# Pair differences of the later batches taken on GpSimd, with three smaller edits, in a fused attention and hardswish kernel

## The chip, the cores and the metric

The kernel runs on one core of a Trainium2 chip. The metric is the device time of one execution in microseconds (us); before the change it was 329.49 us, the median of three runs (325.65 to 331.78). A core has five engines, each with its own in-order instruction queue: TensorE (PE, with its weight loads shown apart as PEld), VectorE (DVE), ScalarE (ACT), GpSimd (POOL) and SyncE (SP). They meet only through semaphores, so an instruction that waits holds back all that is behind it on its engine.

## The reference

`x` has 4 batches of 12480 rows of 128 numbers; `inducing` has 32 rows. All is fp32.

```python
def mab(q, kv):
    s = scale * (q @ kv.transpose(0, 2, 1))
    a = np.exp(s - s.max(-1, keepdims=True))
    a /= a.sum(-1, keepdims=True) + 1e-09
    return a @ kv
h = mab(I, x)              # 32 rows H a batch, from all rows of x
y = mab(x, h)              # each row of x: a weighted mean of those 32 rows
u = y @ w_in               # 128 -> 2048
g = u * np.clip(u + 3.0, 0.0, 6.0) / 6.0
out = g @ w_out            # 2048 -> 128
```

## The kernel before, in words

A row of `y` is a mean of the 32 rows of H with weights p, so `u` is the same mean of the 32 rows of G = H @ w_in. As long as no element of G passes 3 in size, g is the quadratic u (u + 3) / 6, and the square of a mean is the mean of the squares less a sum over pairs of p_m p_n (G_m - G_n)^2. So the kernel never forms `u`. Once a batch it makes a linear matrix L (from hardswish of G) and a quadratic one Cq, with a row for each of 512 features that hold the pairs; each row of the output is then one matmul of its weights with L (through the block matrix BD) and one of its 512 pair products with Cq, divided by its denominator. Conditions that this rests on (sizes of G and of the denominators) are counted as the kernel runs; where one fails, a slow direct path at the end computes everything again.

**Rows.** A batch is 7 groups: 6 of 2048 rows and one of 192. A group is worked on in chunks of 512 rows, 25 chunks a batch, 100 in all.

**What a chunk does (the main loop).** b_base makes the feature exponentials TF in two halves (PE L652, ScalarE L659), two chunks ahead; b_spread loads d, a copy of dk spread over partitions (SP, L639), four ahead; b_prod multiplies the two into TD (VectorE L668), one ahead. Then PE runs b_lin (L676, opens the output bank) and four b_quad (L692, 16 matmuls), with b_r between (L612, denominators, reciprocal on VectorE L613). b_evac (VectorE L708) scales the output one chunk later; SP writes it out a whole group at a time (L715). Once a group b_pack, b_e and b_f (L623, L579, L593) make dk and the normalised weights.

**Preparation of the next batch.** While batch b runs, the units of batch b+1 stand in one list and are woven into the chunks at three points of each (`bg`), a share of the list in proportion to the chunks done. Before the change each unit counts one, whatever it does; some are empty and only space others out. The list has a part on x (a_units): transposes a_T (L260, copied out at L261), scores a_s1 (L268), aggregation a_agg (L282, which also issues the next loads of x on POOL's queue, L118), casts to bf16 (L251). Then comes the coefficient part (c_units):
- c_sum, c_den, c_HT: the softmax sum (dred, L362), H, its transpose HT, rounded copies HTb and HTr, the differences dH of rows of H (VectorE L399, L400), and the coefficients W and Wd of the features.
- c_sq, sixteen times, one for each block jb of 128 columns of w_in: a matmul of dH with w_in (L470) gives the 512 differences of G in PSUM; ScalarE squares them (L481) into `sq`, of which SQB = 12 buffers exist.
- c_G beside it: a matmul of the fp32r HTr with w_in (L414) for G itself.
- c_C, sixteen times: sq times w_out into Cq's bank (L490). It lies twelve units behind c_sq.
- c_hs, c_L, c_BD: hardswish of G, L and BD (L424, L426, L444, L460, L464). c_tail scales Cq (L503, L505).

Batch 0 has nothing to hide under: a_first and c_first prepare it in a row, about the first 46 us.

**End.** After the last chunk's matmuls VectorE counts five conditions (L793 to L806), PE and VectorE add them up into bad_i (L810 to L814), then comes the last b_evac. Every engine loads bad_i and branches over the direct path, whose code is written out four times, once a batch, with three hardware loops in each.

Of the kernel before, what the change touches and what calls it, by code (L numbers as in the profile page):

```python
# [24 lines left out]
TG = 16  # L25
SL = 4
XBUF = 5
SQB = 12
LEAD = 2


def shifted(t, off, k_step, i_step):

    a = t[:, 0, 0:1]
    return bass.AP(
        tensor=a.tensor, offset=a.offset + off, ap=[a.ap[0], [k_step, 2], [1, 32], [i_step, 4]]
    )


@with_exitstack  # L40
def kernel(
# [35 lines left out]
    keep = ctx.enter_context(tc.tile_pool(name="keep", bufs=1))  # L77
    bad_i = keep.tile([1, 1], I32, name="bad_i")

    with ExitStack() as es:  # L80
# [15 lines left out]
        sqp = es.enter_context(tc.tile_pool(name="sqp", bufs=SQB))  # L96
        coef = es.enter_context(tc.tile_pool(name="coef", bufs=2))
        PSUM = bass.MemoryType.PSUM
        psF = es.enter_context(tc.tile_pool(name="psF", bufs=5, space=PSUM))
# [42 lines left out]
        w_in_b = const.tile([P, F], BF16, name="w_in_b")  # L142
        w_in_r = const.tile([P, F], FP32R, name="w_in_r")
        w_out_b = const.tile([P, FB, C], BF16, name="w_out_b")
        w_out_r = const.tile([P, FB, C], FP32R, name="w_out_r")
# [8 lines left out]

        ident = const.tile([P, P], FP32, name="ident")
        make_identity(nc, ident[:, :])
# [146 lines left out]
        def a_units(b):  # L303

            us = []
            late = []
            for g in range(NGR):
                box = {}

                def s1_unit(g=g, box=box):  # L310
                    a_s1(b, g)
                    box["a1"] = S[b]["a1"]

                def first(g=g):
                    a_T(b, g, 0)
                    if g + 1 < NGR:
                        a_cast(b, g + 1, ((nc.scalar.copy, 0, 2),))

                def second(g=g):
                    a_T(b, g, 1)  # L320
                    if g + 1 < NGR:
                        a_cast(b, g + 1, ((nc.scalar.copy, 2, 4),))

                us.append(first)
                if late:
                    us.append(late.pop(0))
                us.append(second)
                us += late
                us.append(s1_unit)
                late = [  # L330
                    lambda g=g, box=box: a_agg(b, g, 0, box["a1"]),
                    lambda g=g, box=box: a_agg(b, g, 1, box["a1"]),
                ]
            return us + late

# [49 lines left out]
        def c_HT(b):  # L385
# [7 lines left out]
            nc.scalar.copy(st["HTb"][:, :], htp[:, :M])  # L393
            st["HTr"] = cst.tile([P, M], FP32R, name="HTr")
            nc.scalar.copy(st["HTr"][:, :], htp[:, :M])
            dH = cst.tile([P, 2, 2, M, 4], BF16, name="dH")
            st["dH"] = dH

            nc.vector.tensor_sub(dH[:, 0], shifted(HT, 0, 1, 0), shifted(HT, 2, 0, 4))  # L399
            nc.vector.tensor_sub(dH[:, 1], shifted(HT, 1, -1, 0), shifted(HT, 4, 0, 4))  # L400
            W = coef.tile([P, 2, M, 4], BF16, name="W")
# [6 lines left out]
        def c_G(b, lo, hi):  # L408
# [4 lines left out]
            for jb in range(lo, hi):  # L413
# [4 lines left out]
                )  # L418

        def c_hs(b):  # L420
            st = S[b]
            gp = st["gp"]
            r6 = cst.tile([P, 512], FP32, name="r6")
            nc.vector.tensor_scalar(r6[:, :], gp[:, :], 3.0, 0.0, op0=ALU.add, op1=ALU.max)  # L424
# [42 lines left out]
        def c_sq(b, jb):  # L467
# [8 lines left out]
            if b == 0 and jb % 4 == 1:  # L476
                d32 = cst.tile([P, 512], FP32, name="d32")
                nc.vector.tensor_copy(d32[:, :], dpm[:, :])
# [29 lines left out]
        def c_units(b):  # L508
            gap = [lambda: None]
            cs = [lambda jc=jc: c_C(b, jc) for jc in range(FB)]  # L510
            ls = [lambda: c_hs(b), lambda: c_L(b, 0), lambda: c_L(b, 1), lambda: c_BD(b)]
            us = [lambda: c_sum(b)] + gap + [lambda: c_den(b)] + gap + [lambda: c_HT(b)] + 3 * gap

            us += [lambda jb=jb: (c_sq(b, jb), c_G(b, jb, jb + 1)) for jb in range(SQB)]
            for jb in range(SQB, FB):
                us += [cs[jb - SQB], lambda jb=jb: (c_sq(b, jb), c_G(b, jb, jb + 1))]
            us += ls[0:1] + cs[4:6] + ls[1:3] + cs[6:8] + ls[3:] + cs[8:]
            return us + [lambda: c_tail(b)]

        def c_first():  # L520
# [13 lines left out]
            for c in range(4):  # L534
                b_spread(0, c)
            load_held(3, len(held))
            for jb in range(3, 7):
                sq(jb)
# [162 lines left out]
        def b_evac(b, c, op):  # L701
# [10 lines left out]
            )  # L712
            if (j + 1) * SL == n:
                r0 = b * N + t0
                nc.sync.dma_start(  # L715
                    out[r0 : r0 + p * n, :].rearrange("(p i) c -> p i c", i=n), ot[:p, :n, :]
                )

# [12 lines left out]
        for b in range(1, B):  # L731
            for i, h in enumerate((0, 2)):
                ahead.setdefault(max((b - 1) * NCK + i - 2, 0), []).append(
                    lambda b=b, h=h: a_cast(b, 0, ((nc.scalar.copy, h, h + 2),))
                )
        evac = None

        def fill(share):

            while queue and done_units[0] < share:  # L740
                queue.pop(0)()
                done_units[0] += 1

        done_units = [0]
        for t in range(total):
            if t % NCK == 0:
                b = t // NCK
                assert not queue
                done_units[0] = 0
                begin, span = t, NCK  # L750
                if b + 1 < B:
                    a_begin(b + 1)
                    queue += ([lambda: None] * 4 if b == 0 else []) + a_units(b + 1) + c_units(b + 1)
                n_units = len(queue)

            def bg(part):
                fill(n_units * (t - begin + part) / span)

# [14 lines left out]
            if t in sums:  # L773
                b_f(*sums[t])
            op = b_lin(bo, co)
            b_quad(bo, co, 0, op)
# [7 lines left out]
            if t + 1 < total:  # L784
                b_r(*divmod(t + 1, NCK))
            b_quad(bo, co, 2, op)
            bg(1.0)
            b_quad(bo, co, 3, op)
            evac = (bo, co, op)

        cnt = cst.tile([P, 5], FP32, name="cnt")
        junk = cst.tile([P, NR], FP32, name="junk")
        nc.vector.tensor_scalar(  # L793
            junk[:, :NR], r_all[:, :, :, :].rearrange("p b c s -> p (b c s)"), 1.0e-16, None,
            op0=ALU.is_ge, op1=ALU.add, accum_out=cnt[:, 0:1],
        )
        nc.vector.tensor_scalar(
            junk[:, : B * NGR], nf_all[:, :], -1.0e-8, None, op0=ALU.is_le, op1=ALU.add, accum_out=cnt[:, 1:2]
        )
        nc.vector.tensor_scalar(  # L800
            junk[:, :B], g_all[:, :], 3.0, None, op0=ALU.is_le, op1=ALU.add, accum_out=cnt[:, 2:3]
        )
        nc.vector.tensor_scalar(
            junk[:, :B], d_all[:, :], 1.0e-20, None, op0=ALU.is_ge, op1=ALU.add, accum_out=cnt[:, 3:4]
        )
        nc.vector.tensor_scalar(  # L806
            junk[:, :B], d_all[:, :], 1.0e30, None, op0=ALU.is_le, op1=ALU.add, accum_out=cnt[:, 4:5]
        )
        cp5 = psF.tile([P, 512], FP32, name="cp5", tag="fb")
        nc.tensor.matmul(cp5[:1, :5], lhsT=ones[:, 0:1], rhs=cnt[:, :])  # L810
        cs = cst.tile([1, 1], FP32, name="cs")
        nc.vector.tensor_reduce(cs[:, :], cp5[:1, :5], axis=AX.X, op=ALU.add)
        good = float(P * (NR + B * NGR + 3 * B))
        nc.vector.tensor_scalar(bad_i[:, :], cs[:, :], good, None, op0=ALU.not_equal)  # L814
        b_evac(*evac)
# [5 lines left out]
    with tc.If(bad > 0, preferred_fallthrough_block=False):  # L821
        direct_path(tc, x, inducing, moe_w_in, moe_w_out, out, scale)


def direct_path(tc, x, inducing, moe_w_in, moe_w_out, out, scale):
    nc = tc.nc
# [9 lines left out]
    with ExitStack() as es:  # L836
        kp = es.enter_context(tc.tile_pool(name="d_keep", bufs=1))
        wk = es.enter_context(tc.tile_pool(name="d_work", bufs=1))
        ps = es.enter_context(tc.tile_pool(name="d_ps", bufs=1, space=PSUM))
        ident = kp.tile([P, P], FP32, name="d_ident")  # L840
        make_identity(nc, ident[:, :])
        w_in = kp.tile([P, F], FP32, name="d_w_in")
# [23 lines left out]

        for b in range(B):
            mx = kp.tile([M, 1], FP32, name="d_mx")
# [6 lines left out]
            nc.vector.memset(Ha[:, :], 0.0)  # L875
            with tc.For_i(b * N, (b + 1) * N, TN) as row:
                xt, xT = load(row)
                s = weights_of(xT)
# [3 lines left out]
            nc.vector.tensor_scalar_mul(nm[:, :], mx[:, :], -scale)  # L882
            with tc.For_i(b * N, (b + 1) * N, TN) as row:
                xt, xT = load(row)
                s = weights_of(xT)
# [17 lines left out]
            nc.vector.tensor_copy(HT[:, :], tr[:, :M])  # L903
            with tc.For_i(b * N, (b + 1) * N, TN) as row:
                xt, xT = load(row)
# [65 lines left out]
```

## Time and profile before

| | us |
|---|---|
| runs | 325.65, 331.78, 329.49; median 329.49 |
| profiled execution: first to last instruction (span) | 321.5 |
| median less that span | 8.0 |
| first L676 matmul of batches 0, 1, 2, 3 | 45.61, 120.03, 194.09, 267.25 |
| last L676 matmul | 310.30 |
| last VectorE instruction's end | 313.74 |

The page gives no time of its own for the profiled execution beyond its span, so what lies around the span is taken from the runs. Between the first L676 matmuls of two batches lie 74.4, 74.1 and 73.2 us: these are batches that carry the next one's preparation. The last batch carries none. A group row of the page reads: line, engine, operation, output from inputs, shapes, count, then busy us and mean ns of one, then the idle time ahead of it on that engine and what ended it. A timeline row reads: start, length, engine, line, operation, count.

### The profile page before, as it was taken

What the parts mean: (1) busy time and instruction counts of PE and PEld (TensorE: products, weight loads), DVE (VectorE), ACT (ScalarE), POOL (GpSimd) and SP (SyncE); (2) the same over time, 40 slices, a digit from 0 to 9 for tenths busy, and PEclk for the clock granted to TensorE, in tenths of its full rate; (3) what the DMA queues carried; (4) which work ended last, traced back from release to release, by engine and by line L of the source; (5) the groups of instructions that cost most, each with busy time, mean ns of one, the idle gap of its engine ahead of it and who ended that gap; (6) DMA issues with size and microseconds to landing.
All of it is one profiled execution on the core that took longest, in us unless ns stands there. A gap on an engine that the chain in (4) does not pass through costs nothing.

```text
span 321.5 us, 9629 instructions
## 1 busy us (share of the span) xinstructions
PE 299.8 (93%) x3934; PEld 234.7 (73%) x3934; DVE 237.5 (74%) x542; ACT 229.4 (71%) x416; POOL 23.3 (7%) x59
## 2 busy tenths in 40 slices
PE   7798998999999998999899998999999999999980
PEld 2695756888677877888678777898777777777760
DVE  2688677788876768788786767797895777878780
ACT  2481789986689669986589759887589757777630
POOL 8150110201000000110000000100000000000000
PEclk9599999999999999999999999999999999999996
DMA  7999399898946444799965345652455246666652
GB/s 222 420 276 272 76 386 329 281 307 285 406 115 197 149 151 98 196 357 332 322 203 181 117 106 178 177 181 77 137 187 191 68 139 210 204 207 197 199 218 75
DMA packets 26487, 67.78 MB, mean 211 GB/s; under 512 B 5153, under 2 KB 19521, under 8 KB 20289
## 3 DMA queue, kind: packets, MB, share of 16 engines
q1 hardware_dynamic: 18160, 38.36, 37.1%
q0 software_dynamic: 8272, 28.71, 29.1%
q8 instruction: 33, 0.54, 0.7%
q14 instruction: 22, 0.17, 0.2%
HBM read 29.77 MB, written 25.56 MB: 172 GB/s over the span
## 4 chain that ended last, share of the span: by engine, by line
PE 75%; DMA 11%; DVE 6%; ACT 3%; issue 2%; POOL 0%; DVEq 0%; POOLq 0%
PE op L692 26%; PE bp L652 12%; DMA d<-dk 8%; PE op L676 6%; PE hnd L282 6%; PE pt L260 5%; PE cp L490 4%; PE dpm L470 4%; DMA xr<-in_x_dram 4%; PE s L268 3%; PE pp L623 2%; DVE xT L261 2%; PE sp L593 2%; PE ep L579 2%; DVE TD L668 1%
## 5 line engine op out<-in xcount | busy, mean ns | idle before, releaser
L659 ACT ACTIVATE TF<-bp 128x512 bf16<-128x512 f32 (+1 forms) x200 | 117.9, 600 | 34.8 <-PE rp L612 21.2
L692 PE MATMUL op<-Cq,TF 128*128 128x128 bf16 (+1 forms) x800 | 109.2, 223 | 0.0
L692 PE MATMUL op<-Cq,TD 128*128 128x128 bf16 (+1 forms) x800 | 106.3, 219 | 0.7 <-DVE TD L668 0.5
L708 DVE TENSOR_TENSOR os<-op,r_all 128x512 f32<-128x512 f32 (+1 forms) x100 | 68.2, 682 | 20.1 <-PE op L692 19.2
L692 PEld LDWEIGHTS <-TF 128*128 128x128 bf16 (+1 forms) x800 | 50.7, 98 | 33.5 <-issue 25.4
L652 PE MATMUL bp<-xT,W 128*128 128x512 bf16 (+1 forms) x200 | 75.1, 376 | 0.0
L668 DVE TENSOR_TENSOR TD<-TF,d 128x1024 bf16<-128x1024 bf16 (+1 forms) x100 | 66.8, 668 | 5.2 <-DMA d<-dk 2.5
L692 PEld LDWEIGHTS <-TD 128*128 128x128 bf16 (+1 forms) x800 | 61.4, 98 | 1.2 <-DVE TD L668 1.0
L676 PE MATMUL op<-BD,nf 128*128 128x512 f32 (+1 forms) x100 | 53.1, 531 | 0.0
L251 ACT CAST xb<-xr 128x1024 bf16<-128x1024 f32 (+1 forms) x47 | 46.0, 1002 | 7.1 <-DMA xr<-in_x_dram 7.1
L481 ACT ACTIVATE sq<-dpm 128x512 bf16<-128x512 f32 x60 | 36.5, 645 | 5.6 <-PE dpm L470 3.7
L261 DVE COPY xT<-pt 128x1024 bf16<-128x1024 bf16 (+1 forms) x56 | 33.8, 616 | 7.6 <-PE pt L260 7.5
L613 DVE RECIPROCAL r_all<-rp 128x4 f32<-128x4 f32 (+1 forms) x100 | 17.7, 177 | 23.9 <-PE rp L612 23.5
L612 PE MATMUL rp<-one,nf 128*128 128x4 f32 (+1 forms) x100 | 34.3, 343 | 0.1
L260 PE MATMUL pt<-ident_b,xb 128*128 128x128 bf16 (+1 forms) x400 | 31.0, 223 | 2.0 <-DVE xb L251 1.5
L282 PE MATMUL hnd<-xr,a 128*32 128x128 f32 x384 | 31.8, 229 | 0.5 <-ACT a L274 0.5
L282 PEld LDWEIGHTS hnd<-xr,a 128*32 128x32 f32 x384 | 25.6, 111 | 2.7 <-issue 2.1
L260 PEld LDWEIGHTS <-xb 128*128 128x128 bf16 (+1 forms) x400 | 24.6, 100 | 3.9 <-DVE xb L251 1.6
L118 POOL DMA_DIRECT2D xr<-in_x_dram x25 | 13.5, 543 | 161.8 <-ACT TF L659 94.4
L490 PE MATMUL cp<-w_out_b,sq 128*128 128x128 bf16 x256 | 24.3, 220 | 0.4 <-ACT sq L481 0.4
L470 PE MATMUL dpm<-dH,w_in_b 128*128 128x512 bf16 x64 | 23.7, 381 | 0.9 <-DVE dH L400 0.5
L630 ACT ACTIVATE dk<-pp 128x512 bf16<-128x512 f32 (+1 forms) x28 | 15.8, 564 | 11.5 <-PE pp L623 10.5
(106 smaller groups left out, 343.7 us busy)
## 6 DMA issues: line engine op xcount, KB each, us to landing
out_dram<-os SPq DMA_DIRECT2D x24, 1024.0 KB, 4.2
xr<-in_x_dram POOLq DMA_DIRECT2D x23, 1024.0 KB, 7.8
d<-dk SPq DMA_DIRECT2D x96, 128.0 KB, 4.1
xr<-in_x_dram POOLq DMA_DIRECT2D x2, 512.0 KB, 4.7
w_in_r<-in_moe_w_in_dram POOLq DMA_DIRECT2D x1, 1024.0 KB, 10.1
w_out_r<-in_moe_w_out_dram POOLq DMA_DIRECT2D x1, 1024.0 KB, 14.4
w_in_b<-in_moe_w_in_dram POOLq DMA_DIRECT2D x1, 512.0 KB, 6.8
w_out_b<-in_moe_w_out_dram POOLq DMA_DIRECT2D x1, 512.0 KB, 12.3
```

The lines of the kernel that those rows point to most:

```text
L251: eng(xb[:p, lo:hi, :], xs[(b, g)][:p, lo:hi, :].bitcast(FP32))
L260: nc.tensor.transpose(pt[:, (i - lo) * p : (i - lo + 1) * p], xb[:p, i, :], ident_b[:p, :p])
L261: nc.vector.tensor_copy(st["xT"][:, t0 + lo * p : t0 + hi * p], pt[:, : (hi - lo) * p])
L282: nc.tensor.matmul(st["hnd"][:M, :C], lhsT=a1[:p, i * M : (i + 1) * M], rhs=xs[(b, g)][:p, i, :], start=(g == 0 and i == 0), stop=(g == NG ...
L470: nc.tensor.matmul(dpm[:, :], lhsT=w_in_b[:, jb * P : (jb + 1) * P], rhs=st["dH"][:, :, :, :, :].rearrange("p q k m i -> p (q k m i)"),)
L490: nc.tensor.matmul(st["cp"][:, k * C : (k + 1) * C], lhsT=sq[:, k * P : (k + 1) * P], rhs=w_out_b[:, jc, :], start=(jc == 0 and k == 0), s ...
L652: nc.tensor.matmul(bp[:, :w], lhsT=st["W"][:, k].rearrange("p m i -> p (m i)"), rhs=st["xT"][:, c0 : c0 + w],)
L659: nc.scalar.activation(st[("x", c)][:, k, :w], bp[:, :w], ACT.Exp, scale=scale)
L668: nc.vector.tensor_mul(u[:, :, :w], t[:, :, :w], d[:, :w].unsqueeze(1).to_broadcast([P, 2, w]))
L676: nc.tensor.matmul(op[:p, :], lhsT=st[("nf", g)][:, j * p : (j + 1) * p], rhs=st["BD"][:, :], start=True, stop=False, skip_group_check=True,)
L692: nc.tensor.matmul(op[:p, s * C : (s + 1) * C], lhsT=T[k][:, s * p : (s + 1) * p], rhs=st["Cq"][:, k, :], start=False, stop=(s == SL - 1 a ...
L708: nc.vector.tensor_mul(ot[:p, j * SL : (j + 1) * SL, :], op[:p, :].rearrange("p (s c) -> p s c", c=C), r_all[:p, b, c, :].unsqueeze(2).to_ ...
```

## The change

Four edits, of which the first reaches furthest.

1. For batches 1 to 3 the 512 differences are no longer a matmul of dH. G is made first (c_G3: three bf16 matmuls of 32 columns a block, with the low parts w_in_l and HTl in place of one fp32r matmul), copied twice side by side to SBUF as G2 (c_Gcopy, VectorE), and c_dG subtracts shifted views of G2 on GpSimd, two instructions of 128x256 a block, into one of two `dg` buffers. c_sqG squares dg on ScalarE, reading SBUF, and writes sq in the old order, that is with a step. Each c_dG stands two blocks ahead of its square, c_C one block behind it. SQB falls to 5. w_in_l is made once, on GpSimd, in c_first. Batch 0 keeps the old way.
2. The units carry weights, and `bg` counts weights. The empty units of the coefficient part go, but for one.
3. The counts move: five at the top of the last chunk but one, one in the last chunk, and bad_i before the last quarter of its matmuls. The writes of the last two groups of batch 3 go out a chunk at a time.
4. The direct path is one hardware loop over the batches, and takes its identity matrix from the main part.

```diff
-SQB = 12
+SQB = 5
...
-                us.append(first)
+                w = 0.46 if groups[g][2] == TG else 0.1
+                us.append((w, first))
                 if late:
-                    us.append(late.pop(0))
-                us.append(second)
-                us += late
-                us.append(s1_unit)
+                    us.append((0.49, late.pop(0)))
+                us.append((w, second))
+                us += [(0.49, u) for u in late]
+                us.append((w, s1_unit))
...
+            if b:
+                HTl = cst.tile([P, M], BF16, name="HTl")
+                nc.vector.tensor_sub(HTl[:, :], HT[:, 0], st["HTb"][:, :])
+                st["HTl"] = HTl
+            else:
+                st["HTr"] = cst.tile([P, M], FP32R, name="HTr")
+                nc.scalar.copy(st["HTr"][:, :], htp[:, :M])
...
+        def c_G3(b, lo, hi):
...
+            for jb in range(lo, hi):
+                for k, (w, h) in enumerate(((w_in_b, "HTb"), (w_in_b, "HTl"), (w_in_l, "HTb"))):
+                    nc.tensor.matmul(
+                        gp[:, jb * M : (jb + 1) * M],
+                        lhsT=w[:, jb * P : (jb + 1) * P],
+                        rhs=st[h][:, :],
...
+        def c_dG(b, jb):
...
+            dg = dgp.tile([P, 2, 2, 4, M], FP32, name="dg")
+            nc.gpsimd.tensor_sub(dg[:, 0], stepped(G2, jb, 0, 1, 0), stepped(G2, jb, 2, 0, 4))
+            nc.gpsimd.tensor_sub(dg[:, 1], stepped(G2, jb, 1, -1, 0), stepped(G2, jb, 4, 0, 4))
...
+        def c_sqG(b, jb):
...
+            nc.scalar.activation(
+                sq[:, :].rearrange("p (a m i) -> p a i m", a=4, i=4),
+                dg[:, :, :, :, :].rearrange("p q k i m -> p (q k) i m"),
+                ACT.Square,
+            )
...
+            us = [(0.3, lambda: c_sum(b)), (0.3, lambda: c_den(b)), (0.5, lambda: c_HT(b))]
+            us += [(0.3, lambda: c_G3(b, 0, 4)), (0.3, lambda: (c_G3(b, 4, 8), c_Gcopy(b, 0, 8), c_dG(b, 0), c_dG(b, 1)))]
+            us += [(0.4, lambda: None)]
+            us += [(0.3, lambda: c_G3(b, 8, 12)), (0.3, lambda: (c_G3(b, 12, 16), c_Gcopy(b, 8, 16)))]
+            ls = {5: lambda: c_hs(b), 7: lambda: c_L(b, 0), 8: lambda: c_L(b, 1), 10: lambda: c_BD(b)}
+            for jb in range(FB):
+                if jb + 2 < FB:
+                    us.append((0.0, lambda jb=jb: c_dG(b, jb + 2)))
+                us.append((0.3, lambda jb=jb: c_sqG(b, jb)))
+                if jb in ls:
+                    us.append((0.3, ls[jb]))
+                if jb:
+                    us.append((0.3, lambda jb=jb: c_C(b, jb - 1)))
+            return us + [(0.3, lambda: c_C(b, FB - 1)), (0.1, lambda: c_tail(b))]
...
+            nc.gpsimd.tensor_sub(w_in_l[:, :], w_in_r[:, :].bitcast(FP32), w_in_b[:, :])
...
+            if b == B - 1 and g >= NGR - 2:
+                nc.sync.dma_start(rows[:, j * SL : (j + 1) * SL, :], ot[:p, j * SL : (j + 1) * SL, :])
+            elif (j + 1) * SL == n:
+                nc.sync.dma_start(rows, ot[:p, :n, :])
...
+            if t == total - 2:
+                counts()
+            if t == total - 1:
+                count(5, r_flat[:, NR - SL :], 1.0e-16, ALU.is_ge)
...
             b_quad(bo, co, 2, op)
+            if t == total - 1:
+                verdict()
             bg(1.0)
             b_quad(bo, co, 3, op)
...
-        for b in range(B):
+        with tc.For_i(0, B * N, N) as b0:
```

## The prediction

> **What bounds the kernel now.** I read the page's engine shares first, then its costliest groups with what ended their idle time, then each batch's stretch in the windows table, then the timeline of the stretch that the change rewrites.
>
> ```profile
> PE 299.8 (93%) x3934; PEld 234.7 (73%) x3934; DVE 237.5 (74%) x542; ACT 229.4 (71%) x416; POOL 23.3 (7%) x59
> ...
> L659 ACT ACTIVATE TF<-bp 128x512 bf16<-128x512 f32 (+1 forms) x200 | 117.9, 600 | 34.8 <-PE rp L612 21.2
> ...
> L708 DVE TENSOR_TENSOR os<-op,r_all 128x512 f32<-128x512 f32 (+1 forms) x100 | 68.2, 682 | 20.1 <-PE op L692 19.2
> ```
> PE is busy 93%. ScalarE and VectorE, at 71 and 74%, are idle mostly because PE has not delivered yet, so PE time removed is span removed, unless a helper becomes late.
>
> ```profile
> 193.80:267.10 73.30, 71.99 (x983) 57.80 (x980) 56.56 (x129) 56.95 (x106) 1.03 (x2) 1.00 0.48 149
> 267.10:310.30 43.20, 42.66 (x525) 32.83 (x523) 36.23 (x86) 31.22 (x57) 0.00 (x0) 1.00 0.63 201
> ```
> The first row is the third batch (columns: stretch, length, then busy PE, PEld, DVE, ACT, POOL, granted clock, DMA share, GB/s), the second the last batch, which prepares no other. A chunk without preparation takes 43.05 us / 24 = 1.79 us (first to last L676 matmul, 267.25 to 310.30). GpSimd does next to nothing.
>
> ```profile
> 236.00 0.38 PE L470 MATMUL dpm<-dH,w_in_b 128*128 128x512 bf16 x1
> 236.03 0.37 PE L414 MATMUL gp<-HTr,w_in_r 128*128 128x32 f32 x1
> 236.25 0.39 PE L652 MATMUL bp<-xT,W 128*128 128x512 bf16 x1
> ...
> 202.69 0.56 PE L268 MATMUL s<-I_T,xT 128*128 128x32 bf16 x16
> 203.09 0.27 PE L692 MATMUL op<-Cq,TF 128*128 128x128 bf16 x2
> ```
> Starts, not durations, give PE's price, since matmuls overlap: a pair of difference and G matmul takes 236.25 - 236.00 = 0.25 us; sixteen 32-column bf16 matmuls take 203.09 - 202.69 = 0.40 us, 0.025 each.
>
> **PE work.** In each of three batches 16 pairs go (16 x 0.25 = 4.0 us) and 48 small matmuls come (L268's shape: 48 x 0.025 = 1.2 us). Net -2.8 us a batch, **-8.4 us**. Bounds: 0 if other engines bind there, -12 if the small ones vanish in waits.
>
> **GpSimd.** It gets 32 subtractions of 128x256 a batch. No row shows one.
>
> ```profile
> L188 POOL CAST blk<-blk_f 128x128 fp32r<-128x128 f32 x1 | 0.3, 293 | 0.1
> ...
> L190 POOL CAST one<-one_f 128x4 fp32r<-128x4 f32 x1 | 0.2, 187 | 0.0
> ...
> L214 POOL IOTA i_of<- 128x1 int32 x1 | 0.6, 619 | 0.0
> ```
> The casts give (293 - 187) / 124 = 0.855 ns an element on 0.18 us fixed. If both inputs are read at once a subtraction takes 0.40 us; if each costs a pass, 0.18 + 2 x 256 x 0.855 ns = 0.62 us; with IOTA's 0.62 us as the fixed part, 1.06 us. I take 0.62, from the two rows nearest in kind: 1.25 us for one block jb. Is that fast enough? By the unit weights the squares run from chunk 15.67 (jb 0) to 24.33 (jb 15): 8.67 chunks x 1.79 = 15.5 us, plus 14 aggregations c_C of 0.22 (3.1) and c_L (1.0), plus 0.23 us a chunk by which the same stage now exceeds its PE sum (2.0; 39.5 us from 227.78 to 267.25 against 36). That is 21.6 us for 14 blocks (two are made ahead), 1.54 a block. 1.25 fits, so **0**. What is late if it doesn't: squares on ScalarE wait for POOL, all TF behind them in that queue wait, and PE stands at c_C one block later, where before the squares had a lead of twelve.
>
> **ScalarE.** Sixteen squares read SBUF, not PSUM; the 128x512 cast from SBUF takes 617 ns, a square 645. Their output is written with a step of four bf16. The nearest strided row is dH (L399, 128x256 with four-element steps in fp32, 584 ns, where 512 straight elements take 683): if the square paid 1.7 times, 16 x 0.45 = 7.2 us, within the 9 us that ScalarE idles from 230 to 267. I take 0; bound +1 us a batch. The Trainium skill ("SBUF — State Buffer", Specifications) wants two hits on each 16-byte line for full rate; these 8-byte steps give two, dH's 16-byte steps one, so by it the square costs nothing more; no run here shows it.
>
> **VectorE.** dH's two (2 x 0.58) go, G's copy (2 x 0.68) and HTl (0.18, as Wd's row) come: +0.4 us a batch, under its 9.6 us idle there: 0.
>
> **Shorter lead in the H chain.** Sum, denominator, H and first G stood one to three empty units apart; now they are neighbours. dred 1.02, rD 0.15, H 0.34, HT 0.22, HTb 0.19, HTl 0.18: 2.1 us, of which PE now waits about 1.1 (L388's 0.6, L470's 0.5, over all batches). PE has 0.5 to 0.6 us of other work between neighbours. Bounds 0 and 1.5 a batch; I take 0.5: **+1.5 us**.
>
> **Weights.** The x part gets 12.67 chunks for 10.67, the coefficient part 12.33 for 14.33. PE's sum is unchanged: 0, bounds -1 and +1 a batch.
>
> **Once only.** w_in_l is 128x2048 on POOL: 0.18 + 2 x 2048 x 0.855 ns = 3.7 us from 41.7, after five loads are issued; POOL's next load comes past 50 us: 0 (bound 0.5 for VectorE). SQB 5: batch 0 lags three squares: 0.
>
> **End.** Counts: VectorE is already 2.78 of 3 us busy from 308 to 311, so 1.4 us of counting moved there delays the evacuations by what it saves after them; PE's verdict matmul also waits for the last count, with the last quadratic matmuls queued behind it: 0, bounds -0.6 and +0.4. SP now issues five writes where two were, with no d load behind them; the last one still leaves after the last evacuation: 0. Behind it:
>
> ```profile
> 313.07 0.67 DVE L708 TENSOR_TENSOR os<-op,r_all 48x512 f32<-48x512 f32 x1
> ...
> 316.00:318.00 2.00, 0.00 (x0) 0.00 (x0) 0.00 (x0) 0.00 (x0) 0.00 (x0) 0.51 0.03 8
> 318.00:320.00 2.00, 0.00 (x0) 0.00 (x0) 0.00 (x0) 0.00 (x0) 0.00 (x0) 0.50 0.08 20
> ```
> From 313.74 to 321.5 nothing computes: the last write lands, the engines branch over the direct path, and 8 to 20 GB/s move with no load or store left, which I read as code. The instructions jumped over fall to a third (PE 257 to 72, VectorE 201 to 58). Bounds 0 and -3.8; I take **-1.5 us**.
>
> **Sum.** 321.5 - 8.4 + 1.5 - 1.5 = 313.1 us of span. The median, 329.49, lies 8.0 above the profiled span (the runs lie 4.2 to 10.3 above); with 8.0: **321.1 us**, -2.5%.
>
> **Rivals.**
> *The shared port.* If VectorE's TD (L668, two SBUF inputs, 0.68 us a chunk) and a subtraction exclude each other, POOL loses 0.68 x 8.67 / 14 = 0.42 us a block: 1.67 against 1.54, 0.13 x 14 = 1.8 us a batch, +5.5: 326.6. For it: POOL would be busy over 80% of that stretch, so TD nearly always meets one. Against: in the trace POOL never computes beside TD. The Trainium skill ("SBUF — State Buffer", Who interferes with whom) says just this: a VectorE instruction with two SBUF inputs and a GpSimd one that reads SBUF hold the port pair by an exclusive lock.
> *GpSimd's fixed cost (slower).* With IOTA's row as the fixed part, 1.06 us each, 2.12 a block, 0.58 x 14 = 8.1 a batch, 345; in the middle, at 1.0 us, 340. It decides from 1.9 us a block, 0.95 a subtraction, where the time passes 336.1. For it: 0.62 us for one column. Against: every other POOL row shows 0.09 to 0.19 fixed.
> *PE was not the bound there.* The 8.4 us turn into waits for ScalarE (56.95 of 73.30 busy): 329.5. Against it speak the idle reasons above.
>
> **Chances.** The sum 0.38 (own range 317 to 325), the port 0.28 (325 to 331), no effect 0.10, fixed cost 0.24 (334 to 346). A measurement here tells 2% from no change, 6.6 us: below 322.9 lie most of the first case and a little of the second, 0.30; above 336.1 most of the last with a bit of PE waiting on a late TD, 0.26; between 0.44. The range 316 to 340 leaves out 0.04 below and 0.1 above.
>
> **What would show it.** L470 at 16 matmuls, and a 128x32 bf16 group of 144 on PE; c_dG rows near 0.62 us; preparing batches near 70.4 us; ScalarE idle on POOL at the squares near zero (port: 2 us a batch, with TD above 0.68; fixed cost: 8); the last VectorE instruction 6 us or so before the end for 7.8. I am wrong if a subtraction takes 0.8 us or more, or if PE's idle grows as its work falls.

## The result and the profile after

| | before | after |
|---|---|---|
| median of the runs taken together (us) | 327.57 (four, 323.96 to 331.78) | 346.26 (four, 344.15 to 351.15) |
| time after / time before | | 1.061 [1.0525, 1.069] |
| profiled execution, span | 321.5 | 349.4 |
| preparing batches, first chunk to first chunk | 74.42, 74.06, 73.16 | 83.66, 83.08, 81.90 |
| last batch, first to last chunk | 43.05 | 42.64 |
| last chunk's first matmul to the end | 11.2 | 9.3 |

The change made the kernel 6% slower. The profiled execution of after is the longest of its four (351.15 us), and starts its chunks 3 us late; the lengths of batches do not hold these 3 us. Each preparing batch is about nine us longer: 9.2, 9.0 and 8.7. The last batch and the end are a little shorter. The two profiled executions lie 27.9 us apart and the medians only 18.7, so a typical execution loses less than nine a batch: against e1 below, whose profiled execution lies at its median, the batches of after are 6.4, 7.4 and 6.8 us longer.

The engine shares of after, from the page:

```profile
PE 303.1 (87%) x3963; PEld 234.2 (67%) x3982; DVE 245.3 (70%) x547; ACT 258.2 (74%) x413; POOL 95.8 (27%) x156
```
PE's share fell from 93% to 87%. ScalarE is busy 258.2 us for 229.4, though it has fewer instructions.

The groups of after that the change touched, by line (columns: busy us, mean ns of one, idle time ahead and what ended it):

```profile
L739 DVE TENSOR_TENSOR TD<-TF,d 128x1024 bf16<-128x1024 bf16 (+1 forms) x100 | 72.4, 724 | 14.5 <-DMA d<-dk 7.6 <-ACT TF L730 6.9
L478 ACT ACTIVATE sq<-dg 128x512 bf16<-128x512 f32 x48 | 63.4, 1351 | 0.0
L471 POOL TENSOR_TENSOR dg<-G 128x256 f32<-128x256 f32 x48 | 39.9, 830 | 0.0
L470 POOL TENSOR_TENSOR dg<-G 128x256 f32<-128x256 f32 x48 | 30.7, 639 | 74.9 <-DVE G L457 45.7 <-ACT sq L478 21.2 <-DVE r_all L684 7.7
```
The square takes 1351 ns where L481 took 645. It never waits (0.0 ahead of it). GpSimd waits for it, 21.2 us, not the other way round. A subtraction takes 639 and 830 ns. TD rose from 668 to 724 ns.

To see which engine bounds the stretch with the squares, the windows table is asked for the last nine chunks of the second batch, in each kernel from that chunk's L676 or L747 matmul on (columns: stretch, length, busy PE, PEld, DVE, ACT, POOL). Before:

```profile
169.84:194.09 24.25, 24.25 (x305) 18.85 (x302) 17.06 (x40) 17.89 (x37) 0.00 (x0) 1.00 0.47 156
```
After:

```profile
185.99:215.53 29.54, 23.49 (x283) 17.34 (x284) 18.53 (x40) 29.17 (x43) 19.64 (x28) 1.00 0.44 144
```
Before, PE is busy for all of the 24.25 us. After, ScalarE is busy for 29.17 of 29.54: it has become the bound, and PE stands for six of them. The end of that stretch, from the timeline of after:

```profile
210.85 1.35 ACT L478 ACTIVATE sq<-dg 128x512 bf16<-128x512 f32 x1
...
211.95 1.16 ACT L730 ACTIVATE TF<-bp 128x512 bf16<-128x512 f32 x2
...
212.66 0.69 DVE L739 TENSOR_TENSOR TD<-TF,d 128x1024 bf16<-128x1024 bf16 x1 [1.16 <-ACT TF L730]
213.00 1.33 ACT L478 ACTIVATE sq<-dg 128x512 bf16<-128x512 f32 x1
214.07 0.68 ACT L701 ACTIVATE dk<-pp 128x512 bf16<-128x512 f32 x1
214.38 0.23 PEld L555 LDWEIGHTS <-sq 128*128 128x128 bf16 x4 [1.90 <-ACT sq L478]
214.39 0.40 PE L555 MATMUL cp<-w_out_b,sq 128*128 128x128 bf16 x4 [1.73 <-ACT sq L478]
```
Squares, TF, and dk stand in one queue, back to back. TD waits for a TF that stood behind a square, and c_C's matmul (PE) waits 1.73 us for the square itself.

### The profile page after: what moved, and what is told of

The parts are those of the page before. It is cut to its first block, busy times and chain, and to the rows that moved or that the text cites. A ratio compares the mean times of both kernels' runs of the same rounds, so it can differ in the third digit from the quotient of the medians.

```text
span 349.4 us, 9791 instructions
## 1 busy us (share of the span) xinstructions
PE 303.1 (87%) x3963; PEld 234.2 (67%) x3982; DVE 245.3 (70%) x547; ACT 258.2 (74%) x413; POOL 95.8 (27%) x156
## 4 chain that ended last, share of the span: by engine, by line
PE 54%; ACT 17%; DMA 15%; DVE 8%; issue 4%; POOL 0%; SPq 0%; ACTq 0%; DVEq 0%; POOLq 0%
PE op L763 18%; DMA d<-dk 11%; ACT sq L478 9%; PE bp L723 8%; PE pt L270 5%; PE hnd L292 5%; ACT TF L730 5%; PE op L747 4%; DMA xr<-in_x_dram 4%; PE cp L555 2%; PE s L278 2%; DVE TD L739 2%; PE pp L694 2%; PE sp L664 1%; DVE xT L271 1%
## 5 line engine op out<-in xcount | busy, mean ns | idle before, releaser
L739 DVE TENSOR_TENSOR TD<-TF,d 128x1024 bf16<-128x1024 bf16 (+1 forms) x100 | 72.4, 724 | 14.5 <-DMA d<-dk 7.6
L763 PEld LDWEIGHTS <-TF 128*128 128x128 bf16 (+1 forms) x800 | 51.9, 99 | 32.6 <-issue 27.0
L723 PE MATMUL bp<-xT,W 128*128 128x512 bf16 (+1 forms) x184 | 70.2, 382 | 2.3 <-ACT TF L730 1.9
L763 PEld LDWEIGHTS <-TD 128*128 128x128 bf16 (+1 forms) x800 | 62.6, 100 | 1.8 <-DVE TD L739 1.6
L478 ACT ACTIVATE sq<-dg 128x512 bf16<-128x512 f32 x48 | 63.4, 1351 | 0.0
L747 PE MATMUL op<-BD,nf 128*128 128x512 f32 (+1 forms) x100 | 54.5, 544 | 0.3 <-DVE os L779 0.3
L470 POOL TENSOR_TENSOR dg<-G 128x256 f32<-128x256 f32 x48 | 30.7, 639 | 74.9 <-DVE G L457 45.7
L471 POOL TENSOR_TENSOR dg<-G 128x256 f32<-128x256 f32 x48 | 39.9, 830 | 0.0
L270 PE MATMUL pt<-ident_b,xb 128*128 128x128 bf16 (+1 forms) x400 | 32.9, 230 | 1.1 <-DVE xb L261 1.1
L555 PEld LDWEIGHTS <-sq 128*128 128x128 bf16 x256 | 15.6, 98 | 25.0 <-ACT sq L478 21.3
L270 PEld LDWEIGHTS <-xb 128*128 128x128 bf16 (+1 forms) x400 | 26.4, 104 | 4.5 <-issue 2.1
```

The lines of the kernel that those rows point to most:

```text
L270: nc.tensor.transpose(pt[:, (i - lo) * p : (i - lo + 1) * p], xb[:p, i, :], ident_b[:p, :p])
L471: nc.gpsimd.tensor_sub(dg[:, 1], stepped(G2, jb, 1, -1, 0), stepped(G2, jb, 4, 0, 4))
L478: nc.scalar.activation(sq[:, :].rearrange("p (a m i) -> p a i m", a=4, i=4), dg[:, :, :, :, :].rearrange("p q k i m -> p (q k) i m"), ACT. ...
L555: nc.tensor.matmul(st["cp"][:, k * C : (k + 1) * C], lhsT=sq[:, k * P : (k + 1) * P], rhs=w_out_b[:, jc, :], start=(jc == 0 and k == 0), s ...
L723: nc.tensor.matmul(bp[:, :w], lhsT=st["W"][:, k].rearrange("p m i -> p (m i)"), rhs=st["xT"][:, c0 : c0 + w],)
L739: nc.vector.tensor_mul(u[:, :, :w], t[:, :, :w], d[:, :w].unsqueeze(1).to_broadcast([P, 2, w]))
```

## The experiments

The theory of the first four runs is that the output step of the square is the cost (0.72 us x 16 = 11.5 us a batch). Its rivals are the reading of SBUF, the port that VectorE and GpSimd share, the H chain and the weights.

**The step taken out of after (e1).**

```diff
...
-                sq[:, :].rearrange("p (a m i) -> p a i m", a=4, i=4),
-                dg[:, :, :, :, :].rearrange("p q k i m -> p (q k) i m"),
-                ACT.Square,
+                sq[:, :], dg[:, :, :, :, :].rearrange("p q k i m -> p (q k i m)"), ACT.Square
```


> The changed kernel with one edit: the square writes its 512 outputs in dg's order, without the step of four bf16 (this leaves the rows of Cq in another order than the features, so the quadratic part belongs to other pairs). Theory A, the stepped write: L478 takes 1.35 us in the changed kernel against 0.62 for the same square from PSUM before, 16 x 0.73 = 11.7 us of ScalarE a batch; without the step it takes 0.62, batches 0 to 2 fall from 82 to 72-74 us, time 0.98 to 1.00 of before. Theory B, the source: the square is slow because it reads fp32 from SBUF that GpSimd has just written; it stays near 1.3 us and the time near 1.06. Theory C, the closer H chain and the weights cost most of it: the square falls to 0.62 but the time stays above 1.03.

Measured: 328.11 us, ratio to before 1.001 [0.996, 1.006]; the whole loss is gone, no gain is left. The groups, and the same last nine chunks of the second batch:

```profile
L737 DVE TENSOR_TENSOR TD<-TF,d 128x1024 bf16<-128x1024 bf16 (+1 forms) x100 | 74.8, 748 | 8.8 <-ACT TF L728 5.1 <-DMA d<-dk 3.6
L471 POOL TENSOR_TENSOR dg<-G 128x256 f32<-128x256 f32 x48 | 37.7, 786 | 0.0
L470 POOL TENSOR_TENSOR dg<-G 128x256 f32<-128x256 f32 x48 | 36.1, 752 | 58.2 <-DVE G L457 44.5 <-DVE r_all L682 7.7 <-ACT sq L478 6.0
L478 ACT ACTIVATE sq<-dg 128x512 bf16<-128x512 f32 x48 | 29.9, 630 | 7.6 <-POOL dg L471 7.2
```

```profile
176.21:199.82 23.61, 22.47 (x283) 17.19 (x284) 18.31 (x40) 20.27 (x42) 20.58 (x28) 1.00 0.50 165
```
A straight square from SBUF takes 630 ns, where batch 0's from PSUM take 609 in the same profile: reading SBUF costs next to nothing. ScalarE is back to 20.27 us of 23.61. With the square short, ScalarE now waits for GpSimd, 7.2 us in all.

**The step moved from the write to the read (e2).** sq is written straight; dg is read with a step of 128 bytes.

> The changed kernel with the step on the other side: the square writes sq straight and reads dg with a step of 32 fp32 (128 bytes). Theory A in its narrow form (only a stepped 2-byte write is slow): 0.62 us a square, time 0.98 to 1.00, as without any step. If any step that gives a 16-byte line fewer than two hits is slow: 1.0 us or more, time 1.03 to 1.08. Theory B: 1.3 us.

Measured: 338.12 us, 1.039 [1.029, 1.049]. The square takes 1123 ns:

```profile
L478 ACT ACTIVATE sq<-dg 128x512 bf16<-128x512 f32 x48 | 53.3, 1123 | 0.4 <-POOL dg L471 0.4
```
Stepped reading costs too, but less.

**The step alone, put on the kernel before (e3).** Differences stay matmuls, in dg's order; batches 1 to 3 write the square with the step, from PSUM.

```diff
...
+                if b:
+                    nc.scalar.activation(
+                        sq[:, :].rearrange("p (a m i) -> p a i m", a=4, i=4),
+                        dpm[:, :].rearrange("p (a i m) -> p a i m", a=4, i=4),
+                        ACT.Square,
+                    )
...
```


> The kernel before with one part of the change alone: in batches 1 to 3 dH is built in the order of dg and the square writes it back with the step of four bf16; everything else, the matmul of the differences and the read from PSUM included, as before. Theory A: these 48 squares take 1.3 us from PSUM too (batch 0's stay at 0.62), 11 us of ScalarE a batch more where it idles 16, time 1.02 to 1.07. Theory B: 0.62 us, 1.00. Theory C: 1.00.

Measured: 354.77 us, 1.086 [1.076, 1.096]. Both forms of the square stand in one profile:

```profile
L488 ACT ACTIVATE sq<-dpm 128x512 bf16<-128x512 f32 x48 | 63.0, 1374 | 4.5 <-PE gp L420 4.3
L494 ACT ACTIVATE sq<-dpm 128x512 bf16<-128x512 f32 x12 | 6.8, 609 | 3.4 <-PE dpm L476 3.2
```
Both read PSUM, with the same count of elements, and take 1374 against 609 ns: the step alone makes a kernel slower than after is. Why it costs this kernel 27 us, more than was expected and more than the 18 between after and e1, was not followed up.

**After without its first edit (e4).** Differences by matmul again; weights, close units, counts, stores and the loop stay.

> The changed kernel with its first part undone: batches 1 to 3 take the differences by matmul of dH again and G by the fp32r matmul, squares read PSUM and write straight, no w_in_l; weights, close H chain, short lag of c_C, counts and direct loop stay. Theory A and B: the square 0.62, time 0.98 to 1.01 (tail 2 us shorter, PE's 8.4 us not saved). Theory C: above 1.03.

Measured: 324.50 us, 0.992 [0.987, 0.996]. So the other edits gain something, and GpSimd's subtraction without the step (e1) loses it again: the means of e1 and e4, taken in the same rounds, lie 2.3 us apart. Runs five to nine ask where.

**Empty units back into the H chain, in e1 and in e4 (e5, e7).**

```diff
-            us = [(0.3, lambda: c_sum(b)), (0.3, lambda: c_den(b)), (0.5, lambda: c_HT(b))]
+            gap = [(0.6, lambda: None)]
+            us = [(0.3, lambda: c_sum(b))] + gap + [(0.3, lambda: c_den(b))] + gap + [(0.5, lambda: c_HT(b))] + gap
```


> The straight square of the first run (Cq's rows in another order than the features), and empty units of weight 0.6 put back between c_sum, c_den, c_HT and the first c_G3. Theory D, the H chain: with neighbours PE stands 1.5 us for H in each batch (H's reciprocal is queued on VectorE behind an evacuation, TD and nf, 0.6 us each), and after it the granted clock falls to half for 3.4 us, 1.7 us more. With the gaps both go: batches 1 and 2 fall from 75.4 to 72 us, no half clock inside the batches, time 0.965 to 0.985 of before. Rival E, the shared port and GpSimd's rate take the saving (TD 0.75 for 0.68, ScalarE 7.2 us on GpSimd): batches stay above 74.5, time 0.995 to 1.005.

> The kernel with the differences by matmul (first part of the change undone), with empty units of 0.6 between c_sum, c_den and c_HT. Theory D: PE's stand for H goes here too, batches 1 and 2 from 74.2 to 72.5, time 0.975 to 0.99 of before. If D is wrong: 0.99 as without the gaps.

Measured: e5 329.15 us, 1.001 [0.997, 1.006]; e7 323.81 us, 0.988 [0.984, 0.991]. In e5 PE's wait at the H transpose fell from 3.0 to 0.5 us, and the third batch to 72.63 us, but the second, which still loads x, is 77.66: there TD starts 3.6 us late, in a stretch where transfers of d take 8.3 to 10.9 us from issue to landing beside loads of x and a store of the output (median 4.2). The wait went, the time did not.

**Features in another order (e6).** The features run as (i, m) instead of (m, i), so that neither square nor dg needs a step; d is then spread by four small writes a chunk in place of one.

> As the run with gaps, with the whole output right: the features themselves go in dg's order (W, dH and the half weights built in it), so the square is straight and nothing is stepped; d is then spread by four DMAs of 32 partitions a chunk, for one of 128. If the four DMAs hide (SP issues 400 for 100, 0.34 to 0.54 us each, up to 216 us of 320 on SP's queue): 0.965 to 0.985. If d comes late, VectorE's TD waits for it more than the 2 us of now: 1.0 or above.

Measured: 373.67 us, 1.140 [1.134, 1.146], a miss. The waits of e6 name the writes:

```profile
DVE TD L742 <- DMA d<-dk: 42.0, 27, 6.7
```
The 384 writes of 32 KB take about 0.7 us of SP's queue each, and TD waits 42.0 us for d. A write lands 2.2 us after its issue at the median, sooner than one of 128 KB, so it is likely the issuing that is late.

**The step moved to GpSimd (e8).** The subtractions write dg in sq's order, fp32 with a step of 16 bytes; the square is straight.

```diff
...
-            dg = dgp.tile([P, 2, 2, 4, M], FP32, name="dg")
-            nc.gpsimd.tensor_sub(dg[:, 0], stepped(G2, jb, 0, 1, 0), stepped(G2, jb, 2, 0, 4))
+            dg = dgp.tile([P, 2, 2, M, 4], FP32, name="dg")
+            to = [dg[:, q].rearrange("p k m i -> p k i m") for q in range(2)]
+            nc.gpsimd.tensor_sub(to[0], stepped(G2, jb, 0, 1, 0), stepped(G2, jb, 2, 0, 4))
...
```


> The changed kernel with the step moved to GpSimd: the subtractions write dg with a step of four fp32 (16 bytes), the square reads and writes straight. Output as the reference's. If GpSimd pays for the step as ScalarE does (twice): 1.3 us a subtraction, 2.6 a block against 1.54 that fit, +15 us a batch, time 1.12 to 1.2. If it does not: 0.63, time 1.00 as with the straight square. In between, at 0.95: 1.04 to 1.07.

Measured: 327.64 us, 0.997 [0.993, 1.001]. The groups of e8:

```profile
L472 POOL TENSOR_TENSOR dg<-G 128x256 f32<-128x256 f32 x48 | 39.0, 812 | 0.0
L471 POOL TENSOR_TENSOR dg<-G 128x256 f32<-128x256 f32 x48 | 37.6, 783 | 55.3 <-DVE r_all L683 51.4 <-ACT sq L479 3.8
L479 ACT ACTIVATE sq<-dg 128x512 bf16<-128x512 f32 x48 | 29.9, 630 | 7.7 <-POOL dg L472 7.4
```
On GpSimd the step costs 0.03 us an instruction (783 and 812 for 752 and 786), and the reference's result is had at e1's time. Its second and third batch in the windows table, below those of the kernel before:

```profile
120.03:194.09 74.06, 72.27 (x980) 57.60 (x979) 56.49 (x128) 57.66 (x106) 3.72 (x7) 1.00 0.67 218
194.09:267.25 73.16, 71.85 (x979) 57.66 (x979) 56.42 (x128) 56.81 (x105) 1.03 (x2) 1.00 0.48 149
...
124.67:199.45 74.78, 69.80 (x990) 55.55 (x995) 59.02 (x129) 58.27 (x106) 27.88 (x39) 1.00 0.67 217
199.45:273.70 74.25, 69.66 (x990) 55.52 (x995) 58.78 (x129) 57.01 (x104) 25.18 (x34) 1.00 0.47 146
```
PE's work did fall: 69.80 and 69.66 us, against 72.27 and 71.85 before. Its idle time grew by more: 5.0 and 4.6 us for 1.8 and 1.3. Two waits make up 2.9 of the third batch's 4.6, one at the H transpose and one at c_C on the square (columns: us in all, times, longest):

```profile
PE htp L399 <- DVE d_all L393: 1.5, 1, 1.5
PE cp L554 <- ACT sq L479: 1.4, 3, 0.9
```

**Both waits taken away (e9).** e8 with the empty units of e5, and c_C two blocks behind the square.

> The kernel after with the step moved to GpSimd (as in the run before of that form), with empty units of 0.6 after c_sum, c_den and c_HT, and each c_C two blocks behind its square instead of one. All of the reference is computed. Theory 'idle': without the costly write the subtraction saves TensorE its 2.2 to 2.6 us a batch and gives it back in two waits that the profile of that form shows in batch 2, 1.5 us of the H transpose on VectorE and 1.4 us of c_C on the square; with both away a preparing batch is about 74.3 - 2.9 = 71.4 us and the median 328 - 9 = 319 us. Rival 'contention': the subtractions share VectorE's port and the x loads share GpSimd's queue, so the waits come back at other places, and the median stays at 326 to 330 us with batches of 73 to 78 us, with x loads or TD named in the waits.

Measured: 328.86 us, 1.009 [1.005, 1.012]. "Idle" falls. The profiled execution took 334.08 us, 5 us above the median, so its lengths are on the long side. PE's wait at the H transpose is 0.5 us, yet the third batch is 73.29 us with PE busy 69.30, and the second 77.30. The waits of e9 on d, then those of e10 (below):

```profile
DVE TD L740 <- DMA d<-dk: 14.0, 8, 3.3
```

```profile
DVE TD L677 <- DMA d<-dk: 4.8, 3, 2.6
```
"Contention" had the time right, and the waits did come back elsewhere. Its causes were not separated; what the trace shows is late transfers. From 145 us on, a 1 MB load of x lands 10.3 us after its issue, and the d issued just ahead of it 10.6 us after; d is asked for four chunks ahead, and TD comes to this one 3.3 us too early.

**The end alone, on the kernel before (e10), and of it the loop alone (e12).**

> The kernel before with the end of the kernel after alone: conditions counted ahead of the last output, the direct path as one loop, the last two groups stored by chunks. Pair differences stay matmuls, units are counted without weights. All of the reference is computed. Theory 'end': the gain of the two matmul forms measured so far (4 us) is the end's, since their span after the last chunk's linear matmul is 7.7 us against 11.1 before: ratio about 0.99, time 3 to 3.5 us under the kernel before. Rival 'units': about half is due to units by weights and the closer chain, and the end alone gives 1.9 us or less, ratio 0.994 to 1.0.

> The kernel before with one edit: the direct path as one hardware loop over the batches, with the identity matrix of the main part. All of the reference is computed. Theory 'code': the span from the last VectorE instruction's start to the end, 8.37 us before and 5.05 with the whole end of the change, falls to 5.0 to 5.2 by this edit alone, and the time by 3.3 us, ratio 0.990. Rival 'counts and stores': the smaller writes by chunks or the conditions counted ahead carry it, and the loop alone leaves 6.9 us or more there (1.5 us, the prediction's term), ratio 0.995 or nearer to 1.

Measured: e10 321.52 us, 0.985 [0.978, 0.993], the lowest ratio of this study, though its interval meets that of e7. Its second and third batch are those of before (74.00 and 73.18 us), and its last chunk's first matmul lies 7.8 us ahead of the end. The first batch is 76.85 us, where before has 74.42 and e12 76.22 with the same main loop: so much does a first batch differ without any change to it. e12: 326.40 against 327.98 us, four runs from 322.53 to 331.50, with no interval, so its time tells nothing. Its profile does. Here are its last evacuation and then that of the kernel before; their spans end at 320.8 and 321.5:

```profile
315.23 0.67 DVE L708 TENSOR_TENSOR os<-op,r_all 48x512 f32<-48x512 f32 x1
```

```profile
313.07 0.67 DVE L708 TENSOR_TENSOR os<-op,r_all 48x512 f32<-48x512 f32 x1
```
8.4 us behind its start became 5.5 by the loop alone, and 5.1 with the whole end (after, e4, e10). In e12 the page's queue q14 (instruction) moves 17 packets in all, in before 22; but e6, which has the loop too, moves 22, so the packets are not shown to be the cause.

**Squares by themselves (e11).** Behind the last output of the kernel before: four times a square of 128x512 from SBUF in each form.

> The kernel before with a stretch of squares put behind its last output, for their durations alone; its time means nothing. Per square of 128x512 fp32 from SBUF on ScalarE. Theory 'two-byte store': what costs is a bf16 write whose neighbours are not adjacent; straight bf16 0.60 to 0.63 us, bf16 with a step of two elements and of four 1.1 to 1.4, the interleaved form of the change 1.35, fp32 straight and fp32 with a step of 16 bytes both near 0.63, fp32 read with a step of 128 bytes and straight write 1.1. Rival 'any step': the fp32 write with a step of 16 bytes is as slow as the bf16 one, 1.3 us. Rival 'step beyond 4 bytes': bf16 with a step of two elements is at 0.63. VectorE's multiplication writing the interleaved bf16 form: 0.6 to 0.7 if the price is ScalarE's own, 1.2 or more if it is the write's on any engine.

```profile
L834 ACT ACTIVATE t<-src 128x512 bf16<-128x512 f32 x4 | 5.6, 1394 | 0.0
L833 ACT ACTIVATE t<-src 128x512 bf16<-128x512 f32 x4 | 5.3, 1316 | 0.0
L851 DVE TENSOR_TENSOR v<-src 128x512 bf16<-128x512 f32 x4 | 5.2, 1303 | 0.1
L840 ACT ACTIVATE f<-src 128x512 f32<-128x512 f32 x4 | 4.4, 1092 | 0.0
L845 ACT ACTIVATE r<-src 128x512 bf16<-128x512 f32 x4 | 4.1, 1037 | 0.0
...
L832 ACT ACTIVATE t<-src 128x512 bf16<-128x512 f32 x4 | 3.0, 761 | 0.0
L839 ACT ACTIVATE f<-src 128x512 f32<-128x512 f32 x4 | 2.7, 681 | 0.0
L831 ACT ACTIVATE t<-src 128x512 bf16<-128x512 f32 x4 | 2.5, 625 | 9.1 <-DVE src L820 9.1
```
bf16 written straight 625 ns (L831), with a step of two elements 761 (L832), of four 1316 (L833), in the change's interleaved form 1394 (L834). fp32 straight 681 (L839), with a step of 16 bytes 1092 (L840). Straight write but a read with a step of 128 bytes: 1037 (L845). VectorE's product in the change's form: 1303 (L851); no straight one stands beside it, but VectorE's straight product of the same shape in before (L479, one input from PSUM) takes 686. "Two-byte store" had the price of bf16 with a step of four right, but a step of two costs only a fifth more, and fp32 pays too. So on ScalarE the price goes with the step: small at 4 bytes, double at 8 in bf16, 1.6 times at 16 in fp32. Steps between these were not run, and VectorE wrote one form only.

## Why the prediction was wrong, point by point

It said 321.1 us (316 to 340); it was 346.26.

**The step that failed: ScalarE, "I take 0; bound +1 us a batch".** Two things in it were wrong. The price: it was taken from dH, by which the square would have paid 1.7 times; it paid 2.1 times, 1351 for 630 ns. That row was of another kind: dH is VectorE's, and its step lies in what it reads, while its output is written straight. On ScalarE the stepped read is the cheaper of the two (e2, 1123 ns). The cover: the prediction laid 7.2 us on "the 9 us that ScalarE idles from 230 to 267", an idle time over all of the preparation's second half. But the squares stand in nine chunks at its end, where e1 shows ScalarE busy 20.27 of 23.61 us without the step; 14 or 15 of the 16 squares lie there, 0.72 us more each, which is 10 us; ScalarE's busy time rises by 8.9 there and fills the stretch. The stretch is 5.9 us longer than e1's, of the 7.4 us by which that batch is longer.

The Trainium skill was cited there: in "SBUF — State Buffer" (Specifications) two hits on each 16-byte line are to give the full rate. Here a step of 8 bytes gives two hits and costs 1316 against 625 ns, and even the interleaved form, in which each line is filled in the end, costs 1394: the trace disagrees for ScalarE's writes, and VectorE's 1303 for 686 points the same way. Four-byte steps (761 ns) come nearer to it.

**PE work, -2.8 a batch.** The work fell by 2.2 to 2.5 us a batch (e8). None of it reached the span. The prediction named the sign for this, PE's idle growing as its work falls, and e8 shows that it happens without the step as well. With the step away, the time (e1, 328.11; e8, 327.64) lies near that of the rival in which PE's work turns into waits, 329.5.

**GpSimd, 0.** Right for after, where ScalarE never waits for a subtraction. A subtraction that meets no TD takes 0.63 and 0.70 us in after, for the 0.62 estimated from the casts; the loss is not GpSimd's, so the slower rival, whose 345 us is close to the 346.26 measured, was near by luck: it had the sign and not the cause.

**The shared port.** The rival's mechanism is real. In e8 a subtraction that overlaps a TD takes 0.88 us, one that doesn't 0.66 to 0.71; TD takes 0.92 us (up to 1.21) with a subtraction beside it and 0.68 without. The Trainium skill ("SBUF — State Buffer", Who interferes with whom) calls this an exclusive lock for the whole instruction; the trace agrees that one delays the other, by less on the mean than a whole instruction. The signs that the prediction gave for this rival, ScalarE idle on GpSimd for 2 us a batch and TD above 0.68, appear once the square is short: 2.4 us a batch and 748 ns in e1. So it is likely one of the costs that make e1 and e8 a draw; its share was not measured.

**Shorter lead in the H chain, +0.5 a batch.** Too small where it struck: PE's wait there is 1.5 us (the upper bound) in two of the three batches of e1, since the reciprocal stands on VectorE behind an evacuation, a TD and a normalisation. But taking it away (e5) did not shorten the kernel.

**Weights, 0.** Not told apart from 0: e4 and e7, with weights, are at 0.992 and 0.988, e10, without, at 0.985; the intervals meet. In the profiles the second and third batches of e4 and e7 are 0.3 to 1.7 us longer than e10's, but these kernels differ in more than the weights.

**Once only, 0.** w_in_l took 4.1 us for 3.7; no wait on it shows, and e8, which has it too, starts its chunks at 45.81 us, as before does at 45.61.

**End, -1.5.** Mis-sized: by the profiles, the branch over the direct path is worth 2.9 us by the loop alone (8.4 to 5.5) and 3.3 with the rest, within the bound of 3.8. In after 1.5 us of this are lost again just ahead of the end: the last TD waits 1.5 us for d, which lands 5.7 us after its issue. So it does in e1, e2 and e8 (5.4 and 5.5 in e9 and e5), while in e4, e7 and e10 it is 3.9 us and nothing waits. Why it lands later with the subtractions stays open.

**Around the span, 8.0.** Wrong: it is 1.75 us (351.15 less 349.4). By that, the profiled execution of before took about 323.3 us, just below the shortest of its runs (323.96 to 331.78); the sum belongs to that time, not to the median.

What stays open: why the subtraction on GpSimd, with the step free (e8) and the two waits gone (e9), is slower than the matmul forms of the same rounds (e8 by 1% than e7, e9 by 2% than e10) though PE has 2 us a batch less to do. The port (TD and subtractions 0.2 us longer where they meet) and d landing late beside the loads of x are seen in the traces; their shares were not measured apart.

## What to carry to other kernels

A rearranged output is a price on the instruction that writes it: cost it by the step in bytes from a row of the same kind, and put it on the engine with slack, as e8 did, or measure it alone first. Idle time covers new work only in the stretch where that work stands, so ask the windows table for that stretch and add the new work to the engine's busy time there. A change of several edits is best judged in parts: here the end alone (e10) did better than all four edits together, and by the profiles most of what it gained at the end came from the loop.

## What the runs showed of the hardware

- A 128x512 square on ScalarE: 625 ns straight, 761 with a 4-byte step, 1316 with 8 bytes, and 1092 for fp32 with 16 bytes, where straight fp32 takes 681; GpSimd's 128x256 fp32 subtraction hardly noticed a 16-byte output step (812 for 786 ns).
- PE's granted clock fell to half for stretches of 3.41 us within batches: once in each preparing batch of e1, behind the waits of the H chain, and not once in the profiled executions of before and e7. After has four of them. A wait alone does not tell: the second and third batch of e8 have the same 1.5 us wait at the H transpose, and the clock stays full.
- Instructions that are never run cost time at the end: with the direct path written once instead of four times, 2.9 us of the last 8.4 went (e12).
- d, 128 KB spread over partitions, lands 4.1 us after its issue at the median, and 10.6 (e9) and 10.9 us (e5) after it beside a 1 MB load and a 1 MB store.
